# Weight loads, masks, dummy matmuls and first-layer groups rearranged in the first eight head pairs of an attention and MLP kernel, and the order of later loads

## The chip, the cores and the metric

The kernel runs on one core of a Trainium2 chip. The metric is the device time of one execution in microseconds (us). Engines: PE (TensorE) does matmuls, ACT (ScalarE) exponentials and the leaky ReLU, DVE (VectorE) and POOL (GpSimd) copies and masks, SP issues DMAs; ACT and POOL issue DMAs too.

## The reference

Eight batches of eight heads, 576 queries each, 64 wide. Each head attends to 16 beacon keys, seen by all queries, and causally to its own 576 keys. The attention's output, laid out as 4608 tokens by 512, goes through two matrices with a leaky ReLU between.

```python
k_all = np.concatenate([beacon_k, k], axis=2)
v_all = np.concatenate([beacon_v, v], axis=2)
scores = scale * np.matmul(q, k_all.transpose(0, 1, 3, 2))
causal[:, Nb:] = np.triu(np.ones((S, S), dtype=bool), k=1)
scores = np.where(causal, -1000000000.0, scores)
a = np.exp(scores)
a /= a.sum(-1, keepdims=True) + 1e-09
x = np.matmul(a, v_all)
h = x @ w_in
out = np.maximum(0.01 * h, h) @ w_out
```

## The kernel before

The work on attention goes by pairs of heads: 32 pairs g, four to a batch. A pair has these steps. **score** (L286) makes transposed scores of both heads in four parts of up to 512 columns, each followed by an exponential on ACT (L306), in two PSUM buffers that the four parts share in turn. **masks** (L310) zeroes what lies above the diagonal with four selects on POOL (L320). **value** (L332), in two halves, multiplies probabilities with values and a column of ones, and DVE divides by the sum (L360, L361). **x_transposes** (L368) turns the result into xT, the first matrix's operand; finish(g) (L526) calls it and notes how many chunks of 512 tokens are ready.

Queries and keys come transposed in two ways. For the first two batches (g below 8) PE transposes them, 36 small transposes a pair, and DVE (or ACT) copies them from PSUM: t_q (L228). Later, POOL permutes a loaded tile (permute, L157), a transposing DMA from SP turns it (turn_pairs, L257), and POOL copies it in order into the operand tiles (in_order, L269). Keys go into two fixed tiles k_bufs, queries into a pool of two.

The matrices work on nine chunks. A group is four 512-wide matmuls: moe1 (L382) makes one of 16 slices of a chunk's hidden layer and ACT applies the ReLU (L394); moe2 (L398) makes a quarter of an output tile of 128 tokens, after four of which DVE copies it (L418) and SP stores it (L420). fill() (L425) issues the next group that may go: alternately of the first and second layer once a chunk's first layer is complete. All these, four PSUM tiles shared, take the place of PE's waits.

Every engine's order is the order in which the program issues, by hand: the loop at L534 runs g from 0 to 34. Pairs below 8 have their own form (L538 to L562), g = 8 a stretch that finishes pairs 5 to 7 and then issues 22 groups in a row (L564 to L588), and from there slots between the steps take groups (L591 to L626). loads(g) (L482) puts loads, casts and preparations ahead of a pair. load_qk and the weights are issued by POOL, which converts fp32 to bf16 on the way; load_v by SP as fp32, with a cast on POOL (cast_v, L221). warm_up (L440) is 34 matmuls on the identity while the first loads are under way.

The softmax here doesn't subtract the row's maximum and nothing guards it: scores larger than these inputs give would overflow.

## Time and profile before

| what | us |
|---|---|
| median of 4 runs (lowest, highest) | 356.48 (356.01, 357.15) |
| profiled execution, whole | 356.2 |
| its span, first to last instruction | 354.5 |
| PE busy | 341.1 |
| ACT busy | 189.2 |
| POOL busy | 201.9 |
| DVE busy | 94.8 |
| first score of pair 0 starts | 8.46 |
| last score of pair 5 ends | 31.95 |
| first group of the first layer starts | 35.62 |
| x transposes of pair 7 end, 8 groups issued | 48.92 |
| first score of pair 8 starts, 30 groups issued | 68.01 |

The span is some 1.7 us shorter than the execution. Busy time of PE is that of pipelined matmuls with modelled ends: at half clock PE looks as busy as at full clock and does half the work, so the granted clock is to be read beside it. An idle time in brackets names what ended it.

### The profile page before, as it was taken

Reading aid. Unit: us, or ns where it says so; the run is one execution under the profiler, and the core shown is the slowest. Engines: PE = TensorE matmul, PEld = TensorE weight load, DVE = VectorE, ACT = ScalarE, POOL = GpSimd, SP = SyncE. Lnnn points to the kernel's source line nnn. Section 1 sums busy time; section 2 is a strip of 40 time slices with the busy share of each in tenths; the row PEclk is TensorE's granted clock in tenths of the full one; section 3 lists DMA queues with packets and bytes.
Section 4 is the critical chain, followed back from the end, with each engine's and each line's share of the span. In section 5 each row is a group of like instructions: output and inputs, shape, how many; then the busy total and the mean of one; then the engine's idle time right before and its main releaser. Section 6 shows DMA issues by size and latency. Waiting matters only on the chain.

```text
span 354.5 us, 7340 instructions
## 1 busy us (share of the span) xinstructions
PE 341.1 (96%) x3002; PEld 173.0 (49%) x3002; DVE 94.8 (27%) x231; ACT 189.2 (53%) x278; POOL 201.9 (57%) x343
## 2 busy tenths in 40 slices
PE   5899999999899999999999999999999999999996
PEld 5566554444454454444444454444444554444444
DVE  2388530102233223212222223222322241000111
ACT  3969754576455873478337843685358303633300
POOL 7699927499899899957695769574431100000000
PEclk9579999999999999999999999999999999999999
DMA  8999999998797976992589256900110011000012
GB/s 169 211 204 147 197 204 184 221 217 137 165 194 115 172 146 128 130 231 41 96 154 222 53 98 121 170 2 1 61 59 2 1 61 59 2 30 30 31 60 88
DMA packets 86929, 40.87 MB, mean 115 GB/s; under 512 B 69872, under 2 KB 82160, under 8 KB 86896
## 3 DMA queue, kind: packets, MB, share of 16 engines
q1 hardware_dynamic: 73456, 26.75, 34.7%
q0 software_dynamic: 13152, 13.34, 25.2%
q8 instruction: 23, 0.38, 0.4%
q10 hardware_dynamic: 288, 0.33, 0.4%
q14 instruction: 10, 0.08, 0.1%
HBM read 37.22 MB, written 9.44 MB: 132 GB/s over the span
## 4 chain that ended last, share of the span: by engine, by line
PE 77%; DMA 9%; POOL 6%; DVE 3%; ACT 2%; issue 2%; SPq 1%; POOLq 0%; ACTq 0%
PE acc L409 32%; PE acc L387 27%; PE sc L297 7%; PE av L351 7%; DMA w_out_sb<-in_moe_w_out_dram 3%; DMA q_raw<-in_q_dram 2%; PE tp L373 2%; PE tp L247 2%; DMA v_raw<-in_v_dram 1%; ACT aT L306 1%; DMA v_raw<-in_k_dram 1%; POOL qT L277 1%; DVE osb L418 1%; POOL kT L277 1%; POOL aT L320 1%
## 5 line engine op out<-in xcount | busy, mean ns | idle before, releaser
L387 PE MATMUL acc<-xT,w_in_sb 128*128 128x512 bf16 x576 | 140.2, 379 | 1.4 <-DVE xT L378 1.4
L409 PE MATMUL acc<-w_out_sb,gT 128*128 128x512 bf16 (+1 forms) x592 | 139.6, 373 | 0.0
L306 ACT ACTIVATE aT<-sc 128x1024 bf16<-128x1024 f32 (+3 forms) x128 | 104.3, 869 | 64.4 <-PE sc L297 64.0
L394 ACT ACTIVATE gT<-acc 128x512 bf16<-128x512 f32 x144 | 85.9, 601 | 79.2 <-PE acc L387 79.2
L409 PEld LDWEIGHTS <-gT 128*128 128x128 bf16 x592 | 53.3, 98 | 58.7 <-issue 6.1
L320 POOL TENSOR_SCALAR_AFFINE_SELECT aT<-aT 128x384 bf16<-128x384 bf16 (+2 forms) x128 | 52.6, 449 | 50.0 <-PE av L351 40.1
L387 PEld LDWEIGHTS <-w_in_sb 128*128 128x128 bf16 x576 | 51.9, 98 | 59.5 <-issue 4.2
L418 DVE COPY osb<-acc 128x512 f32<-128x512 f32 (+1 forms) x37 | 25.0, 677 | 134.7 <-PE acc L409 134.6
L351 PEld LDWEIGHTS <-aT 128*128 128x128 bf16 (+1 forms) x960 | 37.5, 99 | 14.7 <-issue 2.6
L297 PE MATMUL sc<-qT,kT 64*128 64x80 bf16 (+4 forms) x384 | 37.1, 296 | 4.9 <-ACT aT L306 1.8
L351 PE MATMUL av<-v_aug,aT 128*128 128x65 bf16 (+1 forms) x960 | 40.7, 196 | 0.0
L361 DVE TENSOR_TENSOR x_nat<-av,rec 128x384 bf16<-128x384 f32 x64 | 31.4, 491 | 2.2
L224 POOL CAST v_aug<-v_raw 128x512 bf16<-128x512 f32 (+1 forms) x40 | 23.2, 618 | 9.6 <-DMA v_raw<-in_v_dram 9.6
L277 POOL COPY qT<-q_turn 128x576 bf16<-128x576 bf16 x24 | 28.1, 1172 | 0.0
L277 POOL COPY kT<-k_turn 128x576 bf16<-128x576 bf16 x24 | 28.0, 1168 | 0.0
L297 PEld LDWEIGHTS <-kT 64*128 64x128 bf16 x384 | 12.9, 96 | 30.7 <-issue 18.9
L378 DVE COPY xT<-tp 128x576 bf16<-128x576 bf16 x32 | 14.5, 453 | 49.8 <-PE tp L373 49.8
L360 DVE RECIPROCAL rec<-av 128x6 f32<-128x6 f32 x64 | 12.1, 190 | 58.1 <-PE av L351 58.1
L135 POOL DMA_DIRECT2D k_raw<-in_k_dram x31 | 19.4, 624 | 5.5 <-DMA w_out_sb<-in_moe_w_out_dram 5.5
L135 POOL DMA_DIRECT2D q_raw<-in_q_dram x31 | 19.0, 613 | 2.6 <-DMA w_out_sb<-in_moe_w_out_dram 2.5
L164 POOL COPY q_nat<-q_raw 128x1152 bf16<-128x1152 bf16 x12 | 13.8, 1147 | 4.6 <-DMA q_raw<-in_q_dram 4.6
L373 PEld LDWEIGHTS <-x_nat 128*128 128x128 bf16 (+2 forms) x160 | 11.2, 98 | 9.2 <-DVE x_nat L361 2.3
(36 smaller groups left out, 88.0 us busy)
## 6 DMA issues: line engine op xcount, KB each, us to landing
out_dram<-osb SPq DMA_DIRECT2D x35, 256.0 KB, 2.0
v_raw<-in_v_dram SPq DMA_DIRECT2D x24, 256.0 KB, 5.1
q_raw<-in_q_dram POOLq DMA_DIRECT2D x31, 144.0 KB, 5.0
k_raw<-in_k_dram POOLq DMA_DIRECT2D x31, 144.0 KB, 5.1
w_in_sb<-in_moe_w_in_dram POOLq DMA_DIRECT2D x4, 512.0 KB, 6.7
w_out_sb<-in_moe_w_out_dram POOLq DMA_DIRECT2D x4, 512.0 KB, 12.3
v_raw<-in_v_dram SPq DMA_DIRECT2D x8, 224.0 KB, 3.7
v_raw<-in_v_dram SPq DMA_DIRECT2D x8, 160.0 KB, 4.7
```

Source lines behind the costliest of these rows:

```text
L135: dma = nc.gpsimd.dma_start(out=dst[e * RP : (e + 1) * RP], in_=src[b, h0 : h0 + 2].rearrange("h (p i) d -> p h i d", i=RI),)
L224: eng.tensor_copy(out=dst[0 : ROWS[c], c, :, 0:D], in_=t[0 : ROWS[c], c])
L277: nc.gpsimd.tensor_copy(out=dst.rearrange("c (p i) -> c p i", i=RI), in_=t[:, :, e].rearrange("c i p -> c p i"),)
L297: nc.tensor.matmul(out=sc[:, par, col - c0 : col - c0 + w], lhsT=kT[ps_, c * 128 : (c + 1) * 128], rhs=qT[ps_, q0 : q0 + w], start=True, s ...
L306: nc.scalar.activation(out=aT[:, :, c0 : c0 + w], in_=sc[:, :, 0:w], func=AF.Exp, scale=0.125)
L320: nc.gpsimd.affine_select(out=part, in_=part, compare_op=ALU.is_ge, fill=0.0, base=base, channel_multiplier=-1, pattern=pattern,)
L351: nc.tensor.matmul(out=avv[:, n, 0 : D + 1], lhsT=aT[0 : ROWS[c], par, a0 : a0 + 128], rhs=va[0 : ROWS[c], c, 2 * hp + par, :], start=(c = ...
L361: nc.vector.tensor_tensor(out=x_nat[:, t0:t1].rearrange("p t e d -> p (t e) d"), in0=avv[:, :, 0:D], in1=rec[:, n0:n1, None].to_broadcast( ...
L387: nc.tensor.matmul(out=acc, lhsT=w_in_sb[:, j, fc * 128 : (fc + 1) * 128], rhs=xT[:, j, i * 512 : (i + 1) * 512], start=(j == 0), stop=(j ...
L394: nc.scalar.activation(out=gT[i][:, fc, :], in_=acc, func=AF.Prelu, alpha=0.01)
L409: nc.tensor.matmul(out=acc[:, 0:w], lhsT=gT[i][:, fc, t * 128 : (t + 1) * 128], rhs=w_out_sb[:, fc, c0 : c0 + w], start=(fc == 0), stop=(f ...
L418: nc.vector.tensor_copy(out=osb[:, 0:w], in_=acc[:, 0:w])
```

## The change

In the start, POOL loads each weight matrix in two halves of 2 MB of fp32 instead of four quarters; w_in's first half goes between the two halves of batch 1's queries and keys, and batch 1's values wait until the first of these landed. Beacon keys of batches 2 to 7 are loaded after the weights, those of batch 0 and 1 first. A third key tile lets beacon columns be copied ahead, by POOL from pair 2 on. Masks of pairs 0 and 1 become a product with a triangle of ones on DVE. The warm-up is split (24, 18, 4, 3 matmuls), and 14 more follow in each of pairs 0 and 1. The key cast of the first pair is split over ACT and DVE, its copy from PSUM into two parts. x transposes move to the end of a pair. Pairs 6 and 7 have their own order with 13 groups, all of the first layer, and the second layer may start only after 26 groups of the first. From pair 8 on, in_order runs two pairs ahead, behind a pair's scores, and loads and permutes follow its masks. The diff, cut to its core:

```diff
--- before.py
+++ after.py
@@ -95,7 +95,7 @@
             nc.gpsimd.memset(t[:, :, :, D : D + 1], 1.0)

     a_bufs = [singles.tile([128, 2, ACOLS], BF16, name=f"aT{i}") for i in range(3)]
-    k_bufs = [singles.tile([128, NKB * 128], BF16, name=f"kT{i}") for i in range(2)]
...
-    def load_w_in(i):
-        return nc.gpsimd.dma_start(
-            out=w_in_sb[:, :, i * 512 : (i + 1) * 512], in_=w_in_r[:, :, i * 512 : (i + 1) * 512]
-        )
-
-    def load_w_out(i):
-        return nc.gpsimd.dma_start(
-            out=w_out_sb[:, i * 4 : (i + 1) * 4, :], in_=w_out_r[:, i * 4 : (i + 1) * 4, :]
-        )
+    def load_w_in(half):
+        cols = slice(half * DF // 2, (half + 1) * DF // 2)
+        return nc.gpsimd.dma_start(out=w_in_sb[:, :, cols], in_=w_in_r[:, :, cols])
+
+    def load_w_out(half):
+        rows = slice(half * NF // 2, (half + 1) * NF // 2)
+        return nc.gpsimd.dma_start(out=w_out_sb[:, rows, :], in_=w_out_r[:, rows, :])
...
-    def load_qk(b, grp):
-
-
-        qk_raw[b, grp] = (
-            qkpool.tile([128, 2, RI, D], BF16, name="q_raw"),
-            qkpool.tile([128, 2, RI, D], BF16, name="k_raw"),
-        )
-        first = None
-        for e in range(2):
+    def load_qk(b, grp, es=(0, 1)):
+
+
+        if (b, grp) not in qk_raw:
+            qk_raw[b, grp] = (
+                qkpool.tile([128, 2, RI, D], BF16, name="q_raw"),
+                qkpool.tile([128, 2, RI, D], BF16, name="k_raw"),
+            )
+        for e in es:
             if b == 0 and grp == 0 and e == 0:
                 continue
...
-                first = first or dma
-        return first
...
-        load_beacon_k(0, 1, nc.scalar)
+        load_beacon_k(0, 2, nc.scalar)
...
-    first_cast = [singles.tile([RP, 2, RI, D], BF16, name=f"{n}_cast") for n in "qk"]
+
+    first_cast = [
+        natpool.tile([128, RI, 2, D], BF16, name=n)[0:RP].rearrange("p i e d -> p (i e d)").rearrange(
+            "p (h i d) -> p h i d", h=2, i=RI
+        )
+        for n in ("q_nat", "k_nat")
+    ]
...
+    def beacon_columns(g, eng):
+        b, hp = divmod(g, NPAIR)
+        eng.tensor_copy(out=k_bufs[g % 3][:, 0:NB], in_=bkT[:, b, hp])
+
...
-            kT = k_bufs[g % 2]
-            nc.vector.tensor_copy(out=kT[:, 0:NB], in_=bkT[:, b, hp])
+            kT = k_bufs[g % 3]
...
+        parts = 2 if g == 0 and which == 1 else 1
+        for part in range(parts):
+            p = slice(part * RP // parts, (part + 1) * RP // parts)
+            copy(
+                out=dst.rearrange("c (p i) -> c p i", i=RI)[:, p],
+                in_=ps[:, 0:S].rearrange("c (i p) -> c p i", i=RI)[:, p],
+            )
...
+    tri = singles.tile([128, 128], BF16, name="tri")
+
+    def make_tri():
+
+        nc.gpsimd.memset(tri, 1.0)
+        nc.gpsimd.affine_select(
+            out=tri,
+            in_=tri,
+            compare_op=ALU.is_ge,
+            fill=0.0,
+            base=0,
+            channel_multiplier=-1,
+            pattern=[[1, 128]],
+        )
+
+    def masks_by_tri(g):
+
+        aT = probs[g]
+        diag = aT[:, :, 512 : 512 + 3 * 464].rearrange("p e (c x) -> p e c x", c=3)[:, :, :, 0:128]
+        for part, seen in (
+            (aT[:, :, 0:112], tri[:, None, NB:128].to_broadcast([128, 2, 112])),
+            (diag, tri[:, None, None, :].to_broadcast([128, 2, 3, 128])),
+            (aT[0:80, :, 1648:1728], tri[0:80, None, 0:80].to_broadcast([80, 2, 80])),
+        ):
+            nc.vector.tensor_tensor(out=part, in0=part, in1=seen, op=ALU.mult)
...
-        can2 = i2 < NCH and i2 < i1
+        can2 = i2 < NCH and i2 < i1 and done1[0] >= NF + 10
...
-    def warm_up(n):
-
-        ps = ps_one.tile([128, 512], FP32, name="av", tag="one")
+    busy = []
+
+    def keep_busy(n):
+
+        if not busy:
+            busy.append(ps_one.tile([128, 512], FP32, name="av", tag="one"))
         for i in range(n):
-            nc.tensor.matmul(out=ps[:, 0:128], lhsT=ident, rhs=ident, start=True, stop=True)
+            nc.tensor.matmul(out=busy[0][:, 0:128], lhsT=ident, rhs=ident, start=True, stop=True)
...
-        load_beacon_k(1, B, nc.sync)
         load_v(0, after=first)
-        load_v(1)
         make_pads()
+        cast_beacon_k(0, 2, nc.scalar.copy)
+        keep_busy(24)
+        beacon_transposes(0, 2)
+        beacon_columns(0, nc.vector)
+        beacon_columns(1, nc.vector)
+        nc.vector.tensor_copy(out=first_cast[0], in_=first_raw[0])
+        nc.scalar.copy(out=first_cast[1][:, 0], in_=first_raw[1][:, 0])
+        nc.vector.tensor_copy(out=first_cast[1][:, 1], in_=first_raw[1][:, 1])
+        keep_busy(18)
+        t_q(0, 0)
+        keep_busy(4)
+        t_q(0, 1, nc.scalar.copy)
+        keep_busy(3)
+        make_tri()
         make_ones()
-        cast_beacon_k(0, 1, nc.scalar.copy)
-        nc.vector.tensor_copy(out=first_cast[0], in_=first_raw[0])
-        nc.scalar.copy(out=first_cast[1], in_=first_raw[1])
-        cast_beacon_k(1, B, nc.gpsimd.tensor_copy)
+        beacon_columns(2, nc.gpsimd)
         cast_v(0, nc.gpsimd, 0, 1)
-        load_qk(1, 0)
-        cast_v(0, nc.gpsimd, 1, 3)
-        warm_up(34)
-        beacon_transposes(0, 1)
-        t_q(0, 0)
-        t_q(0, 1, nc.scalar.copy)
+        load_v(1, after=load_qk(1, 0))
...
             b, hp = divmod(g, NPAIR)
             if g == 1:
+                beacon_columns(3, nc.gpsimd)
+                cast_v(0, nc.gpsimd, 1, 3)
+                load_w_in(0)
                 cast_v(0, nc.gpsimd, 3, 5)
             elif g == 2:
-                load_qk(1, 1)
+                beacon_columns(4, nc.gpsimd)
             elif g == 3:
-                cast_v(1, nc.gpsimd, 0, 3)
-                load_w_in(0)
+                load_qk(1, 1, (0,))
+                beacon_columns(5, nc.gpsimd)
             elif g == 4:
-                cast_v(1, nc.gpsimd, 3, 5)
-                load_w_in(1)
-                load_w_in(2)
+                load_qk(1, 1, (1,))
+                beacon_columns(6, nc.gpsimd)
             elif g == 5:
-                load_w_in(3)
-                load_w_out(0)
-                load_w_out(1)
-            elif g == 6:
-                load_w_out(2)
-                load_w_out(3)
-            elif g == 7:
-                load_qk(2, 0)
-            elif g >= 2 * NPAIR:
-                if has(g + 1):
-                    in_order(g + 1)
-                if b < B - 1:
-                    if hp == 0:
-                        load_v(b + 1)
-                        load_qk(b + 1, 0)
-                    else:
-                        if hp < 3:
-                            for which in range(2):
-                                permute(b + 1, hp - 1, which)
-                        if hp == 1:
-                            load_qk(b + 1, 1)
-                        else:
-                            turn_pairs(b + 1, hp - 2)
-                    if hp == 3:
-                        cast_v(b + 1, nc.gpsimd)
+                beacon_columns(7, nc.gpsimd)
+            elif g > 2 * NPAIR and b < B - 1 and hp > 1:
+                turn_pairs(b + 1, hp - 2)
+                if hp == 2:
+                    load_v(b + 1)
+
+        def loads_after(g):
+
+            b, hp = divmod(g, NPAIR)
+            if b == B - 1:
+                return
+            if hp == 0:
+                load_qk(b + 1, 0)
+                load_qk(b + 1, 1)
+            elif hp < 3:
+                for which in range(2):
+                    permute(b + 1, hp - 1, which)
+            else:
+                cast_v(b + 1, nc.gpsimd)
...
-            if has(g) and g != 2 * NPAIR:
+            if has(g):
                 loads(g)

-            if g < 2 * NPAIR:
+            if g < 6:

                 score(g, 0)
                 score(g, 1)
-                if has(g - 3):
+                if g < 5:
+                    t_q(g + 1, 0)
+                    t_q(g + 1, 1)
+                    if g in (1, 2):
+                        masks_by_tri(g - 1)
+                if g >= 3:
+                    value(g - 2, 0)
+                if g < 2:
+                    keep_busy(3)
+                score(g, 2)
+                if g < 2:
+                    keep_busy(7)
+                score(g, 3)
+                if g < 2:
+                    keep_busy(4)
+                if g == 2:
+                    value(g - 2, 0)
+                if g >= 2:
+                    value(g - 2, 1)
+                if g >= 3:
                     finish(g - 3)
-                if g == 2:
-                    beacon_transposes(1, B)
-                if g + 1 < 2 * NPAIR:
-                    t_q(g + 1, 0)
-                    t_q(g + 1, 1, nc.scalar.copy if g in (4, 6) else nc.vector.tensor_copy)
-                if g > 2:
-                    value(g - 2, 0)
-                if g == 7:
+                if g > 1:
+                    masks(g)
+                continue
+
+            if g == 6:
+
+                finish(3)
+                for n in range(4):
                     fill()
-                score(g, 2)
-                score(g, 3)
-                if g == 2:
-                    value(0, 0)
-                if g >= 6:
-                    fill()
-                if has(g - 2):
-                    value(g - 2, 1)
-                masks(g)
+                t_q(6, 0)
+                t_q(6, 1)
+                fill()
+                score(6, 0)
+                score(6, 1)
+                fill()
+                score(6, 2)
+                score(6, 3)
+                cast_v(1, nc.gpsimd, 0, 2)
+                load_w_in(1)
+                cast_v(1, nc.gpsimd, 2, 5)
+                load_w_out(0)
+                masks(6)
+                load_w_out(1)
+                load_beacon_k(2, B, nc.gpsimd)
+                t_q(7, 0)
+                t_q(7, 1)
+                fill()
+                fill()
+                value(4, 0)
+                value(4, 1)
                 continue

-            if g == 2 * NPAIR:
-
+            if g == 7:
+                score(7, 0)
+                score(7, 1)
+                value(5, 0)
+                finish(4)
+                score(7, 2)
+                score(7, 3)
+                load_qk(2, 0)
+                masks(7)
+                value(5, 1)
+                value(6, 0)
+                finish(5)
+                value(6, 1)
+                fill()
+                fill()
+                value(7, 0)
+                finish(6)
+                fill()
+                value(7, 1)
+                fill()
+                fill()
+                finish(7)
+                continue
+
+            if g == 8:
                 load_qk(2, 1)
+                cast_beacon_k(2, B, nc.gpsimd.tensor_copy)
                 for grp in range(2):
                     for which in range(2):
                         permute(2, grp, which)
                     turn_pairs(2, grp)
-                load_v(2)
-                in_order(g)
-                cast_v(2, nc.gpsimd)
-                finish(g - 3)
-                value(g - 2, 0)
-                fill()
-                value(g - 2, 1)
-                fill()
-                finish(g - 2)
-                value(g - 1, 0)
-                fill()
-                value(g - 1, 1)
-                fill()
-                fill()
-                finish(g - 1)
-                for n in range(22):
+                    if grp == 0:
+                        load_v(2)
+                while done1[0] + done2[0] < 22:
                     fill()
-                loads(g)
+                beacon_transposes(2, B)
+                while done1[0] + done2[0] < 30:
+                    fill()
+                in_order(8)
+                in_order(9)


             chunks = chunks_with(g - 3) if g - 3 >= 2 * NPAIR else ready[0]
@@ -616,6 +700,8 @@
             if has(g):
                 score(g, 2)
                 score(g, 3)
+                if has(g + 2):
+                    in_order(g + 2)
             slot(4)
             if g - 2 >= 2 * NPAIR and has(g - 2):
                 value(g - 2, 1)
@@ -623,7 +709,10 @@
             slot(6)
             if has(g):
                 masks(g)
+                loads_after(g)
             slot(7)
+            if g == 9:
+                cast_v(2, nc.vector)
         while done2[0] < NCH * NF:
             fill()

```

## The prediction

> **What bounds the kernel now.** I read first the page's slices, then a table of stages, then the timelines of TensorE (PE), ScalarE (ACT) and GpSimd (POOL) in the stages that lose time. The slices, each 8.86 us:
>
> ```profile
> span 354.5 us, 7340 instructions
> ...
> PE   5899999999899999999999999999999999999996
> ...
> ACT  3969754576455873478337843685358303633300
> POOL 7699927499899899957695769574431100000000
> PEclk9579999999999999999999999999999999999999
> ```
>
> PE shows 9 from the third slice on; the start is thin, and PEclk falls to half in the second and third slice, where a 9 is then worth half. So time is gained only where PE waits or runs slowly. The stages (length, then busy time by engine, clock, DMA share, GB/s):
>
> ```profile
> core 0: us, PE busy (x) PEld busy (x) DVE busy (x) ACT busy (x) POOL busy (x), PEclk, DMA share, GB/s
> 8.40:12.00 3.60, 2.86 (x50) 1.64 (x51) 1.50 (x3) 3.11 (x5) 0.54 (x1) 0.63 1.23 231
> 12.00:16.00 4.00, 3.35 (x52) 1.85 (x49) 1.49 (x3) 3.48 (x6) 3.56 (x7) 0.50 1.17 204
> 16.00:20.60 4.60, 4.60 (x83) 3.71 (x81) 3.32 (x7) 3.10 (x4) 4.60 (x11) 0.50 1.17 206
> 20.60:25.10 4.50, 4.19 (x86) 2.81 (x83) 3.44 (x8) 2.85 (x4) 4.50 (x10) 0.74 1.09 195
> ...
> 29.10:32.80 3.70, 3.36 (x83) 2.48 (x83) 3.13 (x9) 3.23 (x5) 2.89 (x6) 1.00 0.84 129
> ...
> 48.90:68.00 19.10, 19.10 (x92) 8.54 (x89) 1.15 (x2) 8.91 (x15) 8.86 (x11) 1.00 1.10 195
> ```
>
> Each of the first rows is one pair of heads. At half clock PE alone fills the 4.60 us row; at full clock a pair takes 3.70 with ACT near full. A mean of 0.63 over 3.60 us is 2.66 us at half, so the clock fell at 9.3; 0.74 over 4.50 gives its return at 23.0. What ACT needs is a row of four exponentials:
>
> ```profile
> 28.19 3.26 ACT L306 ACTIVATE aT<-sc 128x832 bf16<-128x832 f32 x4 [0.17 <-PE sc L297]
> 31.93 3.26 ACT L306 ACTIVATE aT<-sc 128x832 bf16<-128x832 f32 x4 [0.47 <-PE sc L297]
> ```
>
> Thus 3.3 us a pair is the floor; the two idle times say that PE was late. The only two long waits of PE after the start are on POOL, for the keys in order of pairs 11 and 12:
>
> ```profile
> 88.45 0.59 PE L297 MATMUL sc<-qT,kT 64*128 64x512 bf16 x4 [0.48 <-POOL kT L277]
> ...
> 96.35 0.58 PE L297 MATMUL sc<-qT,kT 64*128 64x512 bf16 x4 [1.19 <-POOL kT L277]
> ```
>
> And POOL's queue stands between 45 and 54 us in four loads of Q/K:
>
> ```profile
> 45.01 0.60 POOL L135 DMA_DIRECT2D q_raw<-in_q_dram  x1 [0.53 <-DMA w_out_sb<-in_moe_w_out_dram]
> 47.56 0.60 POOL L135 DMA_DIRECT2D k_raw<-in_k_dram  x1 [1.95 <-DMA w_out_sb<-in_moe_w_out_dram]
> 50.10 0.59 POOL L135 DMA_DIRECT2D q_raw<-in_q_dram  x1 [1.95 <-DMA w_out_sb<-in_moe_w_out_dram]
> 54.24 0.59 POOL L135 DMA_DIRECT2D k_raw<-in_k_dram  x1 [3.55 <-DMA w_out_sb<-in_moe_w_out_dram]
> ```
>
> Each of these waited for the landing of the POOL-issued load eight before it (w_out's first was issued at 34.4 and landed 10.3 later, 44.7).
>
> **What the Trainium skill says.** (1) "TensorE: Matmul & The Clock Gate", Part 1 (the HAM clock gate): the array runs at half clock until a free-running window of about 3.4 us was busy, and falls back after an idle one. The trace agrees: half from 9.3 to 23.0, which is four such windows. (2) The same page, Part 4 (PE-mode transpose): transposes do not count as busy in the same way. The trace fits: 16.0 to 20.6 was 100% busy, about 2.0 us of it transposes, and the clock stayed at half. (3) "DMA: Bandwidth & Descriptors", Issuing engines are not separate DMA queues: loads from all issuers share the same engines. The trace agrees: a v load took 3.5 to 4.7 us alone at 63 to 68 us, and 8.0 to 9.8 beside Q/K loads at 17 to 23 us. (4) "VectorE: DVE Perf Modes", the perf-mode tier table: tensor_tensor in bf16 reaches two elements a cycle. No row here shows it; it prices the new masks below.
>
> **The change part by part.** Unit prices, from starts in the timelines: a group of four 512-wide matmuls 0.864 us; a pair's scores 0.92, values 0.93, x transposes 0.26, Q/K transposes 0.68 (full clock). A group that merely moves earlier gains nothing: PE's sum is fixed. I therefore follow PE to fixed marks and count lost time.
>
> *Head, to the first score (8.46 us now).* Removed: 224 KB of beacon keys from SP at 1.6 us, beside the first q and k, which end the wait (landing 4.8 and 6.0). The beacon's copies (4 of 0.16 to 0.2) now stand ahead of q's cast on DVE, +0.35 there; k's cast of 1.15 is halved over ACT and DVE, -0.5; its evacuation in two parts lets the first score start after one (0.4 instead of 0.64), -0.2. The 24+18+4+3 dummy matmuls at 107 ns (34 took 3.6 us) end at 4.0 and 6.2, before q and k are cast; only the 4 between the transposes cost up to 0.4, which the q copy covers. First score at 8.1, bounds 7.6 to 8.5; first exponential 8.5.
>
> *Pairs 0 to 5.* DVE gives four beacon copies (0.16 to 0.93, waits included) to POOL at 0.2 each and takes the masks of pairs 0 and 1: 1,152 elements at two a cycle of 0.96 GHz is 0.6, and three overheads of 0.15 (a 512-element copy of 0.69 less 0.53) make 1.05 us a pair, an estimate from page (4); at one a cycle 1.65. Pair 2's turn then has 3.7 to 4.3 us of DVE work against 3.3 of ACT, but the turn before has slack: cost 0, bound +1.0. POOL loses 3.2 us of masks (4 of 0.40 twice), its beacon copies wait for scores that are past. ACT loses the key copy of pair 5 (0.65). The x transposes move behind the second values, so they no longer delay the third score (the 0.47 above). If the clock holds: 8.5 + 5 x 3.3 + 1.9 (the first two exponentials of pair 5) + 0.4 (its last score) = 27.3, and I add 0.2 a pair for hand-over (ACT's usual idle 0.15 to 0.21) and 0.4 for pair 0's values, whose last v chunks were cast at 19.2 and should come 1 to 2 us sooner without the beacon load and with batch 1's values gated. **Scores of pair 5 end at 28.7**, against 31.95 now.
>
> *Loads.* POOL's order: w_in's first half at about 16.5, before v(1), which waits on SP for Q/K (1,0), some 19.5; SP has nothing behind it before its transposes. By 30.5 the engines must move 1.18 MB v, 2.1 MB w_in and the second Q/K; now they moved more between 14 and 32.5. So w_in half 0 (need 30.4) and v(1) (need 40.8, value of pair 4) come in time. w_in half 1 is issued after masks(5) and two casts, at 32; 2.1 MB at 2.7 us per MB (landings 36.0, 38.3, 41.0 now) lands near 40 and is needed at 46.5 (ninth group). Cost 0; with no cover it would be stalled one for one. w_out lands near 51, first needed at the 27th group, 64. POOL's last load of Q/K (2,1) waits for the beacon behind w_out, 52; permutes and DMA transposes as now; in_order(8) also needs the beacon columns transposed after group 22 (60): 63.7, needed 67.
>
> *Pair 5 to group 13.* Work: values of 3 (second half) 0.56, six x transposes 1.56, 13 groups 11.2, two Q/K transposes 1.36, scores 1.84, values of 4 to 7 3.7: 20.2. Now from 31.95 the same mark (13 groups, pair 7 finished) is 53.24: 21.3 for 19.3 of work, 2.0 lost. After it more is lost: x of pair 3 comes straight after its values (0.55); pair 6's scores wait for its key copy (0.35) and its fourth for two exponentials behind one group (0.75); pair 7's third and fourth likewise (0.9); x of pair 5 (0.4): 3.0 in all. 28.7 + 20.2 + 3.0 = **51.9**. ACT's 13 group outputs of 0.6 lie beside PE.
>
> *To pair 8.* 17 groups 14.7, six beacon transposes and their copy 0.5: 67.1, against 68.0 now. **0.9 gained.**
>
> *Later batches.* in_order runs two pairs ahead instead of one, and loads follow the masks. Pair 11's and 12's waits, 0.48 + 1.19, should go: a pair there lasts 6.6 us or more, POOL's largest share per pair is 2.5 (in order) + 1.6 + 8 loads of 0.6 = 8.9 once per batch, and two pairs of lead cover it. SP now waits in turn_pairs for the permute just queued, with stores behind it: some 5 us, and three output buffers, one filled every 4.4 us or slower, cover that. **1.67 gained**, bounds 0 to 1.7. From 113 us on PE is full before and after: 0.
>
> Sum: 0.9 + 1.67 = 2.6 from the profiled 356.2 (span 354.5 and 1.7 around it) gives 353.6. The median of the runs, 356.48, is 0.3 above that run: 353.9.
>
> **The rivals.**
> *The clock is not held (slower).* The 14 dummies in each of pairs 0 and 1 count as busy or not; if the clock stays at half to 23.0 as now, a turn of pair 0 is scores 1.94, transposes 1.2, dummies 1.5 = 4.65 us instead of 3.3. Starts 8.1, 12.75, 17.4, 22.4 (pair 2 with values 1.83), then 3.45 each: pair 5 ends at 32.2, pair 8 starts at 70.6, 2.6 late; less 1.67 is +0.9: 357.4, and 359.1 if POOL's two waits stay. It decides from where the clock returns after about 19 us. For it: transposes fill the gaps. Against: the dummies are full matmuls, and the values at 19 us did bring the clock back.
> *The clock falls in one or two windows.* Each costs about 1.1 (a turn of 4.4 to 4.65 against 3.3): 355.0 or 356.1, no change to be seen.
> *Everything is covered.* Head 7.7, turns of 3.3 flat, and only the present 2.0 lost after pair 5: 0.4 + 0.9 + 1.0 more: 351.6. For it: DVE and ACT are both just under full, not over.
> *The moved work buys nothing.* Then only the later waits count: 356.48 - 1.67 = 354.8; it lies within my forecast's spread.
>
> **How the numbers follow.** Forecast 353.9 (with the last rival) 0.45; all covered 0.18; one or two windows 0.20; clock lost 0.17. A measurement of this kernel can tell about 0.3%, 1.1 us. Faster 0.45 + 0.18 + a sixth of the third 0.03 = 0.66; same 0.17 from the third and 0.02 of the last = 0.19; slower 0.15. The range goes from all covered to the clock lost with the mask price at its upper end: 351.0 to 358.0.
>
> **What would show it.** PEclk at 1.0 from 12.8 us on; first score near 8.1; four exponentials every 3.3 to 3.5 us; pair 5's last score by 29; 13 groups by 52; pair 8's scores at 67; no wait on POOL's key copies at pairs 11 and 12. Wrong: half clock beyond 19 us, a wait for w_in at the ninth group, values of pair 4 waiting for v's casts, or in_order late at pairs 8 to 12.

## The result, and the profile after

The changed kernel takes 358.37 us (median of 38 runs, 355.98 to 362.16), the one before 356.97 in the runs beside it (59 runs): a ratio of 1.0042, interval 1.0028 to 1.0056. It is slower by 0.4%; the forecast was 353.9. The profiled execution of after took 357.26. Its slices (8.89 us each), PE, ACT, POOL and the clock:

```profile
span 355.5 us, 7406 instructions
...
PE   8888899997999999999999999999999999999996
...
ACT  3986846663354873378337843686348403633300
POOL 6696638497999797966795779667431100000000
PEclk9999999998999999999999999999999999999999
```

The start no longer shows half clock. The one 8 of PEclk is the tenth slice, 80 to 89 us, and PE's only 7 is there too. PE's timeline holds the marks that were forecast (first score 8.1, 13 groups at 51.9, pair 8 at 67.1), and then shows what was not:

```profile
8.04 0.59 PE L306 MATMUL sc<-qT,kT 64*128 64x512 bf16 x4 [0.22 <-ACT kT L259]
...
51.91 7.93 PE L422 MATMUL acc<-xT,w_in_sb 128*128 128x512 bf16 x36
...
67.01 0.59 PE L306 MATMUL sc<-qT,kT 64*128 64x512 bf16 x4
...
84.96 0.35 PE L386 MATMUL av<-v_aug,aT 128*128 128x65 bf16 x4 [2.52 <-DVE v_aug L227]
85.12 1.90 PE L444 MATMUL acc<-w_out_sb,gT 128*128 128x512 bf16 x4
91.28 0.59 PE L306 MATMUL sc<-qT,kT 64*128 64x512 bf16 x4
...
97.93 0.59 PE L306 MATMUL sc<-qT,kT 64*128 64x512 bf16 x4
```

Pair 8 starts 1.0 earlier than before (68.01). The scores at 91.28 and 97.93 are those of pairs 11 and 12: no idle time stands behind them, where before had 0.48 and 1.19. But pair 8's values wait 2.52 us for VectorE's casts of the value tiles, and the group behind them takes 1.90 where others take 1.03. The table of stages around that wait (length, then busy time by engine, clock, DMA share, GB/s):

```profile
core 0: us, PE busy (x) PEld busy (x) DVE busy (x) ACT busy (x) POOL busy (x), PEclk, DMA share, GB/s
80.00:82.50 2.50, 2.45 (x20) 1.18 (x17) 2.50 (x2) 1.86 (x2) 2.50 (x4) 1.00 1.15 178
82.50:85.00 2.50, 0.04 (x2) 0.04 (x2) 2.50 (x2) 0.00 (x0) 2.50 (x5) 1.00 0.79 182
85.00:87.00 2.00, 2.00 (x10) 0.61 (x11) 2.00 (x3) 0.00 (x0) 1.24 (x2) 0.51 0.85 124
87.00:89.00 2.00, 2.00 (x17) 0.86 (x17) 0.78 (x3) 1.41 (x2) 0.00 (x0) 0.64 0.92 57
```

PE and ACT stand still in the second row, DVE and POOL are both full, and then the clock is at half from 85.0 to 88.4: one window of 3.4 us, worth 1.7 of PE's work. (A window here is such a stretch at half clock.) The chain that ended last runs through DVE there:

```profile
78.64 6.28 DVE v_aug L227 x3
84.92 0.04 issue
84.96 0.35 PE av L386 x4
```

These are three of the five casts of batch 2's values, fp32 to bf16; PE waited for the third. Before, they were on GpSimd ahead of pair 9's copies in order; after, the loop's last two lines put them on VectorE (`if g == 9: cast_v(2, nc.vector)`). The groups, before and after (shortest, median and longest in ns, first and last start):

```profile
L224 POOL CAST v_aug<-v_raw x5: 612/617/617, 66.7 to 70.7; 128x512 bf16<-128x512 f32 x4, 80x512 bf16<-80x512 f32 x1
```

```profile
L227 DVE CAST v_aug<-v_raw x5: 411/1364/3067, 78.6 to 86.1; 128x512 bf16<-128x512 f32 x4, 80x512 bf16<-80x512 f32 x1
```

The shortest cast takes 0.41 us, the longest 3.07. Beside them, on GpSimd's timeline, stand the copies in order of pair 11, pair 9's selects and a permute, without a gap. The second and third cast, and GpSimd:

```profile
79.01 3.07 DVE L227 CAST v_aug<-v_raw 128x512 bf16<-128x512 f32 x1
82.00 2.91 DVE L227 CAST v_aug<-v_raw 128x512 bf16<-128x512 f32 x1
...
79.43 1.25 POOL L286 COPY qT<-q_turn 128x576 bf16<-128x576 bf16 x1
80.54 1.24 POOL L286 COPY kT<-k_turn 128x576 bf16<-128x576 bf16 x1
81.66 1.87 POOL L355 TENSOR_SCALAR_AFFINE_SELECT aT<-aT 128x224 bf16<-128x224 bf16 x4
83.49 1.13 POOL L167 COPY q_nat<-q_raw 128x1152 bf16<-128x1152 bf16 x1
```

The second cast, begun at 79.01, ends at 82.08, 0.30 behind the end of the second copy (81.78); the third ends at 84.91, 0.29 behind the permute's (84.62). The Trainium skill, "SBUF — State Buffer", section Who interferes with whom, says that VectorE and GpSimd share a pair of ports as an exclusive lock: a copy or cast in a two-port mode takes it for the whole instruction, and so does GpSimd; the other stands still. The trace agrees: these casts end about 0.3 us behind the end of a GpSimd instruction, however long they have stood. My theory: these casts, shut out by GpSimd's copies, cost the wait of 2.5 and the window of 1.7 behind it; without them the forecast would stand. Rivals: the casts are slow in themselves or their data come late (the values' last load had landed at 69.2); the loss is the clock's alone; the rearranged start or the longer lead of in_order costs the time.

A half-clock window lowers a run's mean clock by 0.5 x 3.4 / 355.5 = 0.005, so that the clock tells how many a run had; full clock below means none. Of after's 39 executions on record 5 had none (355.98 to 357.07), 12 had one (357.26 to 358.67), 22 two to four (357.89 to 362.16).

### The profile page after: what moved, and what is told of

Same layout as the page of the kernel before. It is cut to its first block, busy times and chain, and to the rows that moved or that the text cites. A ratio compares the mean times of both kernels' runs of the same rounds, so it can differ in the third digit from the quotient of the medians.

```text
span 355.5 us, 7406 instructions
## 1 busy us (share of the span) xinstructions
PE 342.2 (96%) x3045; PEld 173.6 (49%) x3045; DVE 104.6 (29%) x240; ACT 187.6 (53%) x277; POOL 197.3 (56%) x335
## 4 chain that ended last, share of the span: by engine, by line
PE 88%; DVE 6%; ACT 3%; issue 2%; POOL 0%; DVEq 0%; ACTq 0%; POOLq 0%
PE acc L444 35%; PE acc L422 34%; PE av L386 8%; PE sc L306 7%; ACT aT L315 2%; DVE v_aug L227 2%; PE tp L408 2%; PE av L482 1%; DVE osb L453 1%; DVE aT L343 1%; PE tp L253 1%; DVE xT L413 1%; DVE kT L259 1%; DVE qT L259 1%; DVE x_nat L396 0%
## 5 line engine op out<-in xcount | busy, mean ns | idle before, releaser
L422 PE MATMUL acc<-xT,w_in_sb 128*128 128x512 bf16 x576 | 138.8, 379 | 1.4 <-DVE xT L413 1.4
L355 POOL TENSOR_SCALAR_AFFINE_SELECT aT<-aT 128x224 bf16<-128x224 bf16 (+1 forms) x120 | 48.7, 441 | 19.8 <-PE av L386 9.9
L306 PE MATMUL sc<-qT,kT 64*128 64x80 bf16 (+4 forms) x384 | 36.1, 285 | 4.2 <-ACT aT L315 3.3
L227 POOL CAST v_aug<-v_raw 128x512 bf16<-128x512 f32 (+1 forms) x35 | 20.2, 613 | 6.2 <-DMA v_raw<-in_v_dram 6.1
L408 PE MATMUL tp<-ident,x_nat 128*128 128x128 bf16 (+2 forms) x160 | 13.7, 214 | 0.5 <-DVE x_nat L396 0.5
```

The source lines that it names most:

```text
L306: nc.tensor.matmul(out=sc[:, par, col - c0 : col - c0 + w], lhsT=kT[ps_, c * 128 : (c + 1) * 128], rhs=qT[ps_, q0 : q0 + w], start=True, s ...
L355: nc.gpsimd.affine_select(out=part, in_=part, compare_op=ALU.is_ge, fill=0.0, base=base, channel_multiplier=-1, pattern=pattern,)
L408: nc.tensor.transpose(ps[:, q0 : q0 + rows], x_nat[0:rows, t].rearrange("p e d -> p (e d)"), ident[0:rows, 0:rows],)
L422: nc.tensor.matmul(out=acc, lhsT=w_in_sb[:, j, fc * 128 : (fc + 1) * 128], rhs=xT[:, j, i * 512 : (i + 1) * 512], start=(j == 0), stop=(j ...
```

## The experiments

All times are medians, with ratios to the kernel before on the same chip, which took 356.83 to 357.06.

### Where the casts stand

**The casts a pair earlier.**

```diff
-            if g == 9:
+            if g == 8:
                 cast_v(2, nc.vector)
```

> The five casts of batch 2's values stay on VectorE but stand one pair earlier, at the end of pair 8's turn instead of pair 9's (all else as in the changed kernel). Theory (the casts are queued too late on VectorE and are held up there by GpSimd's copies, 3 us for one cast of 0.4, so that pair 8's values wait 2.5 us and the array's clock falls after that wait): the casts run from about 71 to 78 us, still stretched, but are over before 82; no wait of TensorE there, and the time falls by 2.5 us and part of a clock window (1.7): 354.0 to 355.5, faster than the kernel before by 0.4 to 0.8%. Rival (v's transfers land late, because their loads stand behind a transposing DMA): the casts end at the same time as now and nothing changes, 358. Rival (the start or later batches lose the time): the wait goes, but the time stays above 357.

354.18 (19 runs), ratio 0.9932, interval 0.9911 to 0.9952: this one digit is worth 4.2 us. The casts are still stretched, 0.60 to 1.40 each, but they end at 80.2 and nobody waits.

```profile
75.66 4.50 DVE L227 CAST v_aug<-v_raw 128x512 bf16<-128x512 f32 x5
```

**The casts on ScalarE, at the same place.**

```diff
             if g == 9:
-                cast_v(2, nc.vector)
+                t, dst = v_raws[2], v_bufs[0]
+                for c in range(NKB):
+                    nc.scalar.copy(out=dst[0 : ROWS[c], c, :, 0:D], in_=t[0 : ROWS[c], c])
```

> The five casts stand where the changed kernel has them, at the end of pair 9's turn, but on ScalarE instead of VectorE. If GpSimd's copies are what stretches the casts on VectorE, ScalarE does them at about 0.6 us each, from 78.5 to 81.6, and pair 8's values wait 0 to 0.3 us: 354.0 to 355.5. If the place alone is at fault, or the landing of v, the wait stays near 2 us: 357.5 to 358.5.

353.67 (6 runs), ratio 0.9924, interval 0.9902 to 0.9947. Casts and pair 8's values:

```profile
80.77 2.69 ACT L717 CAST v_aug<-v_raw 128x512 bf16<-128x512 f32 x5
...
84.38 0.54 PE L386 MATMUL av<-v_aug,aT 128*128 128x65 bf16 x12
```

Started later than VectorE's, they end earlier: 0.62 to 0.63 each, beside GpSimd's DMA issues and beside its copies alike.

**The casts on GpSimd**, behind the copies of pair 9.

```diff
                 in_order(9)
+                cast_v(2, nc.gpsimd)
...
-            if g == 9:
-                cast_v(2, nc.vector)
```

> The five casts go back to GpSimd, behind the copies in order of pairs 8 and 9, where GpSimd now sits idle from 66 to 71 us. Theory: 0.6 us each as in the kernel before, done as v lands (70 to 71), pair 10's copies in order start at most 1 us later; no wait at pair 8's values: 354.0 to 355.5. If later batches' GpSimd order is what costs, a new wait shows on its key copies at pairs 10 to 12.

355.16 (12 runs), ratio 0.9952, interval 0.9927 to 0.9976. No wait at pair 8's values either. Its five runs with full clock took 353.31 to 354.05, like those on ScalarE (353.51 to 353.71); the rest of the median is windows in the start, of which below.

**Only the neighbour taken away.** The casts stay on VectorE where the change puts them, and pair 11's two copies in order leave GpSimd for ScalarE.

```diff
-            nc.gpsimd.tensor_copy(
+            (nc.scalar.copy if g == 11 else nc.gpsimd.tensor_copy)(
```

> The changed kernel, casts on VectorE at the end of pair 9's turn as there, but pair 11's two copies in order on ScalarE instead of GpSimd. It tests what stretches the casts. Theory (VectorE's cast and GpSimd's copy shut each other out): with these copies gone from GpSimd only its masks and permutes are left beside the casts; the second cast, 3.07 us in the changed kernel, falls below 1.6, the five end near 83 instead of 86.5, and pair 8's values wait under 1 us: 354.5 to 356.5. Rival (the casts wait for something else, a semaphore or the landing of v): the second cast still takes 3 us and the wait stays 2.5: 358.

353.78 (6 runs), ratio 0.992, interval 0.9889 to 0.9951.

```profile
79.45 4.53 DVE L227 CAST v_aug<-v_raw 128x512 bf16<-128x512 f32 x5
```

The same five casts on the same engine at the same place take 4.5 instead of 7.9 us, and pair 8's values (82.72) don't wait. The cast itself is neither slow nor late: its neighbour makes it so. What is left of the stretch falls beside the selects and permutes, which stayed. In the five profiles with these casts on VectorE, sixteen take 0.59 to 3.07 us beside a copy, select or permute; all sixteen end 0.28 to 0.33 us behind the end of one of these, as a lock would have it and mere sharing would not.

**This part alone, in the kernel before.**

```diff
                 in_order(g)
-                cast_v(2, nc.gpsimd)
...
                 masks(g)
             slot(7)
+            if g == 9:
+                cast_v(2, nc.vector)
```

> The kernel before with one part of the change alone: batch 2's five value casts go from GpSimd (ahead of the copies in order of pair 9) to VectorE at the end of pair 9's turn. VectorE is free for them at 78.3 us (its output copy of 77.65 ends there), GpSimd has copies in order of pair 10 and permutes from about 75 to 82, and pair 8's values begin at 82.9. If GpSimd's copies stretch the casts wherever they meet, the first casts take 0.7 us or more, the five 4 to 6 us instead of 2.0, and pair 8's values wait 0 to 2 us. GpSimd gains 3.1 us of queue, so the waits of 0.48 and 1.19 for key copies (pairs 11 and 12) may go: 355.5 to 358.5 in all, according to which is larger. Rival: the stretch comes only with the lead of two pairs; then the casts take 2.0 us, no wait, and with GpSimd freed 355.0 to 355.8.

355.72 (20 runs), ratio 0.9963, interval 0.9943 to 0.9983.

```profile
81.12 3.42 DVE L224 CAST v_aug<-v_raw 128x512 bf16<-128x512 f32 x5
```

Stretched (0.54 to 1.00), so the rival's 2.0 us is wrong, but all five take less than the 4 to 6 us expected: they met a permute only until 81.8, then GpSimd's DMA issues, and pair 8's values, at 85.77, did not wait. GpSimd's 3.1 us less of queue took the waits for key copies at pairs 11 and 12 away. The edit that loses 4 to 5 us in after gains 1.3 in before: which instructions it meets decides.

### The wait and the clock behind it

**44 matmuls on the identity in the wait**, so that PE isn't idle.

```diff
+            if g == 10:
+                still = ps_one.tile([128, 512], FP32, name="av", tag="one")
+                for i in range(44):
+                    nc.tensor.matmul(out=still[:, 0:128], lhsT=ident, rhs=ident, start=True, stop=True)
```

> The changed kernel with 44 matmuls on the identity (2.5 us) in front of pair 8's values, so that TensorE is busy instead of waiting there; the casts are as late as in the changed kernel. It separates the wait from the clock that falls after it. Theory: the 2.5 us stay lost, but no window at half clock follows at 85 us (1.7 us in the profile): 356.5 to 357.5. If the clock's windows lie elsewhere (in the start), no change: 358 to 358.5.

357.96 (9 runs), ratio 1.0055, interval 1.0027 to 1.0083: no better than after (1.0042). The window behind the wait is gone in its profile, but two stood in the start, and the wait itself can't be filled. Its four runs with full clock took 357.06 to 357.96, about 1 more than after's five. So the wait, not the clock, is the larger part: after's runs without a window lie 2.8 above those of the casts on ScalarE (medians 356.4 and 353.6), close to the wait of 2.5. The other 2 or so of the 4.7 between the medians are windows.

**No dummy matmuls in pairs 0 and 1** (casts on ScalarE).

```diff
-                if g < 2:
-                    keep_busy(3)
...
-                if g < 2:
-                    keep_busy(7)
...
-                if g < 2:
-                    keep_busy(4)
```

> The kernel with the casts on ScalarE, without the 28 dummy matmuls in the turns of pairs 0 and 1 (the 49 ahead of the first score stay). Theory (the dummies hold the array's clock through pairs 0 to 2): the clock falls at about 9 us and returns near 20 as in the kernel before; pair 2's turn with its first values runs at half and pair 8's scores start 1 to 2.5 us later: 354.7 to 356.2. Rival (ScalarE bounds these pairs and half a clock is hidden): the clock falls in the record, and the time stays at 353.5 to 354.2.

353.99 (6 runs), ratio 0.9915, interval 0.9886 to 0.9945: as fast as with them. The clock did fall, as these rows show:

```profile
12.00:16.00 4.00, 3.21 (x77) 1.99 (x70) 2.51 (x6) 3.85 (x6) 4.00 (x8) 0.58 1.03 191
16.00:20.00 4.00, 4.00 (x78) 2.72 (x76) 3.96 (x7) 2.58 (x4) 4.00 (x9) 0.57 1.02 141
```

Two windows at half clock, and pair 3's scores begin at 18.62, against 18.41 in after; counted from each one's first score that is 10.9 and 10.4, so 0.5 later. In the first row ACT is full: PE at half clock has room behind it. The theory that the dummies carry the start fell. The kernel before says the same: among its 38 executions beside the experiment with the casts alone, ten at a mean clock of 1.0 took 355.90 to 357.39, three at 0.966 (seven windows) 357.23 to 357.79: seven windows for some 0.8 us.

**More dummies, in pairs 2 to 5** (casts on ScalarE).

```diff
+                if 3 <= g < 6:
+                    keep_busy(4)
                 score(g, 2)
...
+                if 2 <= g < 6:
+                    keep_busy(6)
                 score(g, 3)
```

> The kernel with the casts on ScalarE, with dummy matmuls in the turns of pairs 2 to 5 as well (6 ahead of the fourth score, 4 ahead of the third from pair 3 on), where TensorE waits 0.2 to 0.5 us for ScalarE. Theory (windows at half clock between 17 and 31 us come from these waits): fewer executions with such windows, and a median at or 0.5 below that of the same kernel without them, 353.0 to 353.7. Rival (these pairs are already full, and the PSUM tile that the dummies hold is missed): later, 354 to 355.

354.85 (16 runs), ratio 0.9958, interval 0.9931 to 0.9984. 10 of 16 runs had no window, and even these took 353.74 to 355.91. Nothing is gained.

### The lead of in_order

**One pair of lead instead of two**, ahead of a pair's scores as in the kernel before (casts on ScalarE).

```diff
                 in_order(8)
-                in_order(9)
...
+            if has(g + 1):
+                in_order(g + 1)
             if has(g):
                 score(g, 0)
...
-                if has(g + 2):
-                    in_order(g + 2)
```

> The kernel with the casts on ScalarE, with GpSimd's copies in order one pair ahead, ahead of a pair's turn as in the kernel before, instead of two pairs ahead behind its scores; loads and permutes stay as changed. Theory (two pairs of lead remove the waits at pairs 11 and 12): waits of TensorE on the key copies come back at pairs 10 to 12, 1.5 to 3 us in all: 355.0 to 356.7. If the lead does nothing and the order of loads does it: no waits, 353.5 to 354.2.

356.59 (22 runs), ratio 0.998, interval 0.996 to 0.9999. The waits for key copies are back, at pairs 10 and 14:

```profile
81.90 0.59 PE L306 MATMUL sc<-qT,kT 64*128 64x512 bf16 x4 [0.89 <-POOL kT L286]
...
110.08 0.59 PE L306 MATMUL sc<-qT,kT 64*128 64x512 bf16 x4 [0.94 <-POOL kT L286]
```

0.89 + 0.94 = 1.8, beside the 1.67 that the prediction gave the second pair of lead. The runs without a window differ by the same 1.8 (medians 355.4 and 353.6); between the medians of all lie 2.9, windows included.

### The masks of pairs 0 and 1

In four of these profiles (three with the casts moved, and the 44 matmuls) one to three half-clock windows stand between 19 and 31 us. The exclusion is at work there too: pair 1's three mask products on VectorE begin at about 17, beside GpSimd's last value casts and pair 2's selects. With the casts on ScalarE:

```profile
16.76 3.66 DVE L343 TENSOR_TENSOR aT<-aT,tri 128x224 bf16<-128x224 bf16 x3
...
16.60 1.18 POOL L227 CAST v_aug<-v_raw 128x512 bf16<-128x512 f32 x2
...
17.95 1.60 POOL L355 TENSOR_SCALAR_AFFINE_SELECT aT<-aT 128x224 bf16<-128x224 bf16 x4
...
21.18 0.78 PE L386 MATMUL av<-v_aug,aT 128*128 128x65 bf16 x12 [1.79 <-DVE x_nat L396]
```

VectorE's division of pair 0 stands behind the products, and pair 1's values behind that. By themselves the products take 0.88, as where GpSimd stood idle in the profile with the casts on GpSimd:

```profile
17.04 0.88 DVE L343 TENSOR_TENSOR aT<-aT,tri 128x224 bf16<-128x224 bf16 x3
...
18.64 0.61 POOL L227 CAST v_aug<-v_raw 80x512 bf16<-80x512 f32 x1 [1.63 <-DVE x_nat L396]
```

The idle time ahead of that cast, and PE's 1.80 behind it, are not the exclusion's, although the view names VectorE: the last of batch 0's value loads landed at 18.59. The profiles without the two copies and with the 44 matmuls have the same, with landings at 18.20 and 17.72 and the cast at 18.26 and 17.77. The last one's view says so:

```profile
17.77 0.73 POOL L227 CAST v_aug<-v_raw 80x512 bf16<-80x512 f32 x1 [0.35 <-DMA v_raw<-in_v_dram]
```

In after the same load landed at 16.81.

**These masks back on GpSimd** (casts on ScalarE).

```diff
                     if g in (1, 2):
-                        masks_by_tri(g - 1)
+                        masks(g - 1)
```

> The kernel with the casts on ScalarE, and the masks of pairs 0 and 1 again as four selects each on GpSimd, at the same place in the order, instead of products on VectorE. The products took 1.8 and 2.0 us a pair where 1.05 was priced. If VectorE's time there bounds pair 2's turn, or shuts GpSimd out of its value casts, taking them away brings pair 8's scores 0.3 to 1 us earlier: 352.7 to 353.4. Rival: ScalarE sets the pace of the start and the products are hidden; GpSimd takes 3.2 us more instead, its w_in load and value casts come later, and the time is 353.5 to 354.7.

358.22 (20 runs), ratio 1.0034, interval 1.0014 to 1.0053. Both expectations missed: it is 4.5 slower. Pair 0's values wait, and PE runs at half clock from 17.6 to 27.8, three windows:

```profile
19.33 0.77 PE L386 MATMUL av<-v_aug,aT 128*128 128x65 bf16 x5 [2.08 <-POOL aT L355]
```

```profile
18.00:22.00 4.00, 2.36 (x32) 1.84 (x34) 0.88 (x3) 0.19 (x1) 4.00 (x11) 0.50 1.05 176
22.00:26.00 4.00, 4.00 (x74) 2.80 (x71) 2.56 (x6) 2.66 (x4) 3.44 (x9) 0.50 1.13 201
```

ACT, with 0.19 in four us, waits for PE here, so that this half clock is not hidden; pair 8 starts at 72.2. In the changed order, then, the masks on VectorE are worth 4.5 us, stretched or not.

**Pair 1's products left out** (casts on ScalarE; pair 1 keeps what lies above the diagonal).

```diff
-                    if g in (1, 2):
-                        masks_by_tri(g - 1)
+                    if g == 1:
+                        masks_by_tri(0)
```

> The kernel with the casts on ScalarE; the three mask products of pair 1 on VectorE are left out, so pair 1's probabilities keep what lies above the diagonal. In the profiles so far these products start at about 17.0 us, beside GpSimd's last value casts and the selects of pair 2, and took 0.88, 2.0, 2.5, 2.8, 3.6, 3.7 or 3.8 us. Theory: this is the same exclusion of VectorE and GpSimd, and the waits of TensorE it makes at 18 to 22 us (0.9 to 1.8) are what lets the clock fall there in about half of the runs. Without them no wait of over 0.6 us between 17 and 23, nearly all runs at a mean clock of 0.995 or more, median 353.0 to 353.5. Rival: the windows come from elsewhere (the many small transposes, ScalarE's waits); then a third to a half of the runs still has a mean clock of 0.99 or less, and the median stays at 353.7 to 355.

353.05 (6 runs), ratio 0.9903, interval 0.9875 to 0.9931. No wait over 0.5 between 17 and 23, five of six runs without a window, pair 8 at 67.17 (69.48 with them, in a profile with one window).

**Two DMA issues ahead of pair 2's selects** (casts on ScalarE).

```diff
             elif g == 3:
-                load_qk(1, 1, (0,))
...
+                if g == 2:
+                    load_qk(1, 1, (0,))
                 if g > 1:
                     masks(g)
```

> The kernel with the casts on ScalarE; the two loads of Q/K of batch 1's second half that stand behind pair 2's selects on GpSimd go ahead of them, so that GpSimd issues DMAs (1.2 us) where VectorE wants to multiply pair 1's masks. Theory: the products, at 17 us, then lose at most the last value casts (until 17.8) and end by 19.0 instead of up to 20.4; TensorE's wait of 1.8 at pair 1's values goes, fewer runs have half-clock windows, median 353.2 to 353.7. Rival: the selects, 1.2 us later, delay pair 2's values, or the earlier loads delay w_in: 353.9 to 355.

353.28 (6 runs), ratio 0.9909, interval 0.9882 to 0.9937; five of six runs without a window.

```profile
17.17 2.06 DVE L343 TENSOR_TENSOR aT<-aT,tri 128x224 bf16<-128x224 bf16 x3
...
18.43 0.60 POOL L133 DMA_DIRECT2D q_raw<-in_q_dram  x1
...
19.62 1.61 POOL L355 TENSOR_SCALAR_AFFINE_SELECT aT<-aT 128x224 bf16<-128x224 bf16 x4
```

The products end at 19.2 instead of 20.4, pair 1's values (19.98) don't wait, pair 8 starts at 67.22. It is the fastest kernel with all of the work, though its interval covers that of the casts on ScalarE alone.

Ten profiles are of after or of variants that keep the dummies in pairs 0 and 1 and have no masks of these pairs on GpSimd. In six of them PE waited 0.65 to 1.80 between 17 and 22 us. In three (casts a pair earlier, casts on ScalarE, one pair of lead; 1.62 to 1.79) it waited for VectorE's division behind stretched products: that the exclusion makes these waits is shown. In the other three (0.65 to 1.80) it waited for the late load named above. Half clock followed in two of each three, and in none of the four profiles with waits of 0.41 or less. So windows go with waits, but the exclusion makes only a part of the waits. That it accounts for the share of runs with windows is not shown: 10 of 12 had none in the last two kernels, 4 of 6 with the casts on ScalarE alone, too few to tell apart.

## Why the prediction was wrong

**What held.** First score 8.04 (8.1), 13 groups 51.91 (51.9), pair 8 67.01 (67.1). The 51.9 has some luck in it: pair 5's scores ended at 28.1 instead of 28.7, and the stretch behind them took 23.8 instead of 23.2. No wait for w_in at the ninth group, none at pair 8's start. Pairs 11 and 12 don't wait; the lead is worth 1.8 (1.67), though it is not the only cure: in the kernel before, the casts' leaving GpSimd took both waits away without it, and no term of the prediction says so. With the casts earlier, on ScalarE, or away from pair 11's copies the kernel takes 353.67 to 354.18 around the forecast of 353.9.

**The step that failed.** "Later batches" costed the lead of in_order and the order of loads and stopped: the sum, "0.9 + 1.67 = 2.6", has no term for the last lines of the diff, five casts that join VectorE's queue at the end of pair 9. That put them at nothing without a reason. Five of the shortest would have been 5 x 0.41 = 2.0 us (an estimate), in place by 80.7, before pair 8's values at 81.9: nothing. Beside what the change itself moves to this place on GpSimd (the copies of a pair two ahead) they took 7.9, and the third, for which PE waited, was in place at 84.9. Against the prediction's sum of 353.6, after's profile has + 2.5 (the wait) + 1.7 (half clock behind it) = 357.8; it took 357.26. The 0.5 between is made up after 111 us; where is not known.

**A second place with the same error.** The masks were priced at 1.05 us a pair, "cost 0, bound +1.0". Alone they take 0.88: that price was near. Beside GpSimd they took 1.2 to 3.75. In after's own profile (1.80 and 2.01) it cost nothing; in three others it made PE wait 1.62 to 1.79. The prediction compared VectorE's work with ScalarE's time per pair and took two engines' queues for independent.

**The rivals.** "The clock is not held" gives 357.4 and so comes near the measured time, for a wrong reason: this profile's clock held in the start and fell at 85. Its price falls as well: without dummies two windows at half clock put pair 3's scores 0.5 later and left the median at 353.99. Two windows, ACT full in the first, were all but hidden there; the one at 85 us in after, ACT idle for most of it, was worth 1.7. The prediction's 1.1 for each knew no such difference.

The page on the clock gate (the Trainium skill, "TensorE: Matmul & The Clock Gate", Part 1) puts the fall after an idle window of about 3.4 us. Here less was enough: 2.5 us without matmuls at 85.0 and a wait of 1.79 near 21 us in two profiles, while one of 1.62 there in another brought no fall. The free-running window that the prediction named does show: the changes of clock in a profile lie multiples of 3.41 us apart (in after at 6.53, 85.03 and 88.45). How busy PE was in the 3.4 us up to a change goes with it but does not decide alone: 0.9 us before the fall at 85.0, 1.6 and 2.2 before those at 21.3 and 21.0; yet with one pair of lead the wait of 1.62 lay across such a point at 20.0, left 2.8 and 2.1 on its two sides, and the clock held. The limit stays open.

The prediction also read value loads a little narrowly: alone they took 3.5 to 5.1 us, beside Q/K loads 6.9 to 9.8. No term rests on that.

## What to carry to other kernels

In these runs a cast or a two-input product on VectorE had no fixed price while GpSimd copied, selected or cast in SBUF: lay the two engines' timelines over one another before pricing either, and when a change moves GpSimd's work, look again at every VectorE instruction that now falls beside it. If a deadline hangs on such a step, ScalarE (0.63 a cast here, the same beside GpSimd) or a place one step earlier was safer than the engine that is quickest by itself. And cost every line of a diff, the last two above all: what no term of the sum names is not free.

## What the runs showed of the hardware

- VectorE's cast of 512 columns, fp32 to bf16, took 0.41 us at its shortest and 3.07 across two GpSimd copies of 1.25. The stretched ones ended 0.28 to 0.33 us behind the end of a GpSimd instruction, and the longest stood through two copies in a row, or through selects and a permute. GpSimd lost little in turn: the copies took 1.25 instead of 1.17, a permute 1.33 instead of 1.14.
- Beside GpSimd's DMA issues four such casts took 0.54 to 0.74 each: slower than 0.41, far from shut out.
- One wait of 2.5 us on PE was followed by a window of 3.4 us at half clock, which cost two thirds as much again. The clock changed only at multiples of 3.41 us; how much of such a stretch must be idle for a fall is not shown.
